# Weight sums of the last era made ahead of the spectral stage, query tiles kept from gate sums to output, and spectral visits that begin with five free banks

## The chip, the cores and the metric

The kernel runs on one core of a Trainium2 chip. The metric is the device time of one execution in microseconds (us). Before the change the median of three runs is 385.83 us (385.55 to 385.86). The engines are PE (the matrix engine), DVE, ACT and POOL (vector, activation and general engines) and SP, whose queue issues nearly all transfers.

## What is computed

One sequence of S = 2048 tokens with D = 512 channels, in fp32. Cut to what matters:

```python
def _A_ref(q, k, v, shift_k, ssm_k, ssm_D):
    for t in range(4):                                   # short causal convolution of k
        k_shift += pad(k, 3)[:, t:t + S, :] * shift_k[:, 3 - t]
    kv = k_shift * v
    y = irfft(rfft(pad(kv, S)) * rfft(pad(ssm_k, S)))[:S]    # long convolution, length 2 S
    return q * (y + kv * ssm_D)

def _B_ref(x, w1, w2):                                   # w1 512 x 1792, w2 1792 x 512
    return relu(x @ w1) @ w2

x = A_q
g = sigmoid((x * gate_w).sum(-1, keepdims=True))         # one gate per token
return g * _A_ref(x, ...) + (1 - g) * _B_ref(x, w1, w2)
```

## The kernel before

**Two halves on one PE.** The MLP (`_B_ref`) takes most of PE's time. A product in fp32 is made of three matmuls: each operand is split into a high part (an ACT cast) and a low part (`split`, L300 to L312: the low part is one subtraction on DVE, or on POOL), and high x high, high x low and low x high are added up in PSUM. Of `mlp1` these are L385 to L387 (m<-xh/xl, w0), of `mlp2` L607 to L609 (m<-w1, hh/hl). A dense matmul takes 128 partitions and 512 columns. The 14 blocks of the hidden width are worked in three eras (blocks 0 to 4, 5 to 9, 10 to 13), each over four chunks of 512 tokens; the partial output of an era is kept in y tiles (L617, L622). The last era makes `x @ w1` by a seven-product scheme (`combine`: products X, V and Y in L458 to L460). It needs sums of quarters of the inputs (t1 to t4, L408, tiles r_b and xs_b) and of the weights: s1 = a21+a22, s2 = s1-a11, s3 = a11-a21, s4 = a12-s2, made by `load_combined` (L543, tiles raw_s) and split like any weight (w0l_l_s; the last quarter a22 in L562).

**The convolution** is a transform in two levels, in 64-row matmuls on tiles of PE that stand between the dense ones as "visits". Eight visits of stage 1 (L652) write the array sa in device memory. Then come the spectral visits (`conv_mid`): visit g reads group g of sa and has, in this order, the inverse of group g-2 (iv, L839, four PSUM banks), the transform of the filter (f_h, two and two banks) and of the signal (f_x, two and two banks; L765). There are eight, and two more (here iv6 and iv7) that have the inverse alone. ACT copies iv out (bv, L849, then stored to sb) and half of f_h (L792); DVE makes the other half of ha from f_h (L797), multiplies it with f_x (p of 2048 columns, then ha, qa, qb, ha of 1024 columns, L805), and POOL adds these products into p (L811, eight sums of 512 columns a group; four of group 7 on DVE). p is what the inverse reads two visits later. Four visits of `conv_end` (cy, L918) read sb, and `after` and `finish` (L928, L864) multiply by q and the gates, add y and store the output.

**Gates.** `gates` loads q a second time in eight tiles gq of 512 KB and makes sixteen row sums with one DVE instruction each (L883), then one sigmoid on ACT and 1-g on DVE. This happens during stage 1; the spectral stage's memory opens only when it is over. `conv_end` loads each q tile once more (tag q), and the output has tiles o.

**What sets the order.** Nothing is ordered by the hardware. `Plan` collects all instructions with a duration, a rank, the buffers and PSUM banks (eight, called cv) that they take and give, and plays them through; the order in which it starts them is written out, and each engine runs its list in that order. A DVE or POOL instruction that waits therefore holds all that stand behind it on its engine, and a PE matmul that waits for a bank holds PE. A visit is a chain on PE that nothing may enter. Its first link starts in the plan if it can take its own banks; a `need` asks for more free banks than it takes, for at most PATIENT = 20 us of the plan, and only the cy visits use it (NEED = 4):

```python
if op["need"] and not live and op["asked"] > now - PATIENT and op["need"] > sum(o is None or o.get("over", False) for o in line["cv"]):
    continue
```

The iv link of every visit carries `pair` 4, whose patience is 0 (LONG), so it starts with the four banks that it takes. Ring r has eight tiles of 512 KB, used in turn by loads of stage 1, of the spectral groups, of the first half of the last era's inputs and of sb.

Of the kernel before, what the change touches and what calls it, by code (L numbers as in the profile page):

```python
# [14 lines left out]
P = 128  # L15
NF = DFF // P
NCHUNK = 4
NJ = 32
# [53 lines left out]
class Plan:  # L72
# [24 lines left out]
    def order(self):  # L97
# [157 lines left out]
def build(tc, wf, xp, qn, kn, vn, hn, dn, sh, gw, w1, w2, cs1, ccf, cci, cib, out):  # L255
# [12 lines left out]
    sb = dram.tile([P, 32, D], F32, name="sb")  # L268


    room = {"raw": RAW, "x": 4, "cv": 8, "hh": HB, "o": OB, "cc": BEHIND + 1, "cf": 2, "qa": 1, "qb": 1, "acc": ACC, "tmp": TMP, "ev": EV, "r": RB,
            "ha": HAB, "p": PB, "bv": BVB, "j": 1, "q": QB, "w1": WA, "w2": WB, "xs": 4, "gq": 2}
# [123 lines left out]
    def combine(p, c, d, cgate):  # L396
        pairs = [tuple(ERAS[2][2 * u:2 * u + 2]) for u in range(2)]
        rank = (1, XR[p])
        tag = "xs" if p else "r"
        raws, made = {}, {}  # L400
        for nm, src, k0 in (("b22", d, 2), ("b12", d, 0), ("b11", c, 0), ("b21", c, 2)):
            go = lambda nm=nm, src=src, k0=k0: nc.sync.dma_start(rows(tile_of(("xc", p, nm), tag, 2 * D, p=cpool[0] if p else mp)), xp[src, k0:k0 + 2].rearrange("k p d -> p k d"))
            raws[nm] = add("SP", ISSUE, (-47, rank[1])[p], go, [cgate if p else xgate[0]], [tag], dma=2 * ROW, fifo=[tag])
# [27 lines left out]
        def again():  # L431
            nc.sync.dma_start(rows(tile_of(("xc", p, "b22"), "xs", 2 * D)), xp[d, 2:4].rearrange("k p d -> p k d"))

        for nm, ld in (("t2", "t4"), ("t3", "t2"), ("t4", "t4"), ("t1", "t2"), ("b22", None)):
            if not ld:
                made[ld] = add("SP", ISSUE, rank[-1], again, [cgate, made["t2"]], ["xs"], dma=2 * ROW, fifo=["xs"])
            for i in range(2):
                cut(nm, i, made[ld], [tag if ld else "xs"] if i else [])
# [80 lines left out]
        begun[0] = p5[1]  # L519
# [4 lines left out]

    def load_combined(rank):
        tt = lambda eng: (nc.gpsimd if eng == "POOL" else nc.vector).tensor_tensor
        H = 256
        for u in range(2):
            f, g = ERAS[2][2 * u], ERAS[2][2 * u + 1]
            lf = loaded(("w", 0, f), w1[f], rank - 3 + u, mp)  # L530
            lg = loaded(("w", 0, g), w1[g], rank - 3 + u, mp)
            T["wr", u] = f, g
            own = split(("w", 0, f), "w0", (1, rank + u), lf, WA, wp, ["w1"], ())[1]
            wpart["a11", u] = wpart["a12", u] = own
            ops = {}

            def combo(nm, half, a, b, sign, deps, take=(), give=(), u=u):
                def go(eng="DVE"):
                    key = ("wc", "s12" if nm in ("s1", "s2") else "s34", u)
                    if take:  # L540
                        tile_of(key, "raw", p=mp)
                    part = lambda q: T["w", 0, T["wr", u][q[0]]][:, H * q[1]:H * q[1] + H] if len(q) == 2 else T["wc", "s12", u][:, H * q[0]:H * q[0] + H]
                    tt(eng)(T[key][:, H * half:H * half + H], part(a), part(b), op=OP.add if sign > 0 else OP.subtract)  # L543

                return add("DVE", dve_time(H), (1, rank + u), go, deps, take, give, port=True, alt=("POOL", 0.68), fifo=take)
# [6 lines left out]
            hi, lo = ("wc", "h", "a"), ("wc", "l", "a")  # L552

            def h(u=u, g=g):
                if not u:
                    tile_of(hi, "w0h", dt=F32R, bufs=WA, p=wp)
                nc.scalar.copy(T[hi][:, H * u:H * u + H], T["w", 0, g][:, H:])

            def l(eng, u=u, g=g):
                if not u:  # L560
                    tile_of(lo, "w0l", dt=F32R, bufs=WA, p=wp)
                tt(eng)(T[lo][:, H * u:H * u + H], T["w", 0, g][:, H:], T[hi].bitcast(F32)[:, H * u:H * u + H], op=OP.subtract)  # L562

            for nm, ld in (("s34", s4), ("a", s3), ("s12", s4)):
                if nm == "a":
                    a = add("ACT", act_time(H), (1, rank + u), h, [lg, ahigh[0]], [] if u else ["w1"], fifo=[] if u else ["w1"])
                    ahigh[0] = a
                    wpart["a22", u] = add("DVE", dve_time(H), (1, rank + u), l, [a, s3, alow[0]], (), ["raw"], port=True, alt=("POOL", 0.68))
                    alow[0] = wpart["a22", u]
                else:  # L570
                    own = split(("wc", nm, u), "w0", (1, rank + u), ld, WA, wp, ["w1"], ["raw"])[1]
                    for q in nm[1:]:
                        wpart["s" + q, u] = own

    ahigh, alow = [None], [None]
# [172 lines left out]
    def conv_mid(g, gate):  # L748
# [6 lines left out]
        def link(dur, fn, deps, take, give=(), pair=0):  # L755
            o = add("PE", dur, (0, rank), fn, (deps if not chain else [chain[-1]]), take, give, tiles=True, pair=pair)
            chain.append(o)
            return o
# [16 lines left out]
        for o in [old]:  # L775
            if o >= 0:
                put_iv(o, link(2 * TILES, lambda o=o: inverse(o), deps, ["cv"] * 4, ["p", "cc"], 4))
        if g >= NJ // 4:
            plan.chain(chain)
            return  # L780
        planes = lambda z, u, n=2: T[k(z)][:, u * D:(u + n) * D].rearrange("p (r d) -> p r d", d=D)
        ha, fh = [], []
        for o in range(2):
            f = link(TILES, lambda o=o: rounds("h", o), deps, ["cv"] * 2 + ([] if o else ["ha"]), rtags[g, "h"] if o else ())
            fh.append(f)

# [68 lines left out]
    def finish(n, key, rank, deps, give):  # L855
        parts = 2 if n == LAST else 1
        prev = None
        for i in range(parts):
            z = slice(i * D // parts, (i + 1) * D // parts)

            def go(z=z):
                if z.start == 0:
                    tile_of(("o", n), "o")
# [3 lines left out]
            prev = add("DVE", dve_time(D // parts) + 0.06, (*rank, i), go, deps + [prev], [] if i else ["o"], give if last else (), port=n // 4 not in DIRECT)  # L867
            add("SP", ISSUE, 0, lambda z=z: nc.sync.dma_start(out[:, n, z], T["o", n][:, z]), [prev], (), ["o"] if last else (), dma=ROW // parts)
# [4 lines left out]
    def gates():  # L873
        gwl = add("SP", ISSUE, GATE - 3, lambda: nc.sync.dma_start(tile_of(("gwt",), "gwt"), gw.partition_broadcast(P)), [sload[0]], dma=ROW)
        prev = []
        for n in range(0, 16, 2):
            key = ("gq", n)
# [213 lines left out]
```

## Time and profile before

| | before |
|---|---|
| median of three runs | 385.83 us |
| the profiled execution, its own time | 385.63 us |
| its span (first to last instruction) | 383.9 us |
| PE busy | 377.8 us, 2481 matmuls |
| DVE, ACT, POOL busy | 298.6, 170.2, 89.4 us |
| bytes moved | 99.84 MB |

The time of the profiled execution is its span and 1.7 us around it. Each row of the timeline gives the start from the span's beginning, the duration, engine, line, operation, output<-input, and the shape; rows "x32" join one stretch of equal matmuls. Matmuls overlap, so the distance from start to start is what one of them costs, not its duration. In brackets stands idle time of the engine before the row and what ended it.

### The profile page before, as it was taken

Reading aid. Unit: us, or ns where it says so; the run is one execution under the profiler, and the core shown is the slowest. Engines: PE = TensorE matmul, PEld = TensorE weight load, DVE = VectorE, ACT = ScalarE, POOL = GpSimd, SP = SyncE. Lnnn points to the kernel's source line nnn. Section 1 sums busy time; section 2 is a strip of 40 time slices with the busy share of each in tenths; the row PEclk is TensorE's granted clock in tenths of the full one; section 3 lists DMA queues with packets and bytes.
Section 4 is the critical chain, followed back from the end, with each engine's and each line's share of the span. In section 5 each row is a group of like instructions: output and inputs, shape, how many; then the busy total and the mean of one; then the engine's idle time right before and its main releaser. Section 6 shows DMA issues by size and latency. Waiting matters only on the chain.

```text
span 383.9 us, 6643 instructions
## 1 busy us (share of the span) xinstructions
PE 377.8 (98%) x2481; PEld 269.7 (70%) x2481; DVE 298.6 (78%) x383; ACT 170.2 (44%) x311; POOL 89.4 (23%) x71
## 2 busy tenths in 40 slices
PE   9999999999999999999999999989999999999995
PEld 5888877877877876886645565565778887668864
DVE  5698999999699774258878987999987718979262
ACT  5642356176156547142134253324228854268410
POOL 1000000000000000000988899969620000000000
PEclk9999999999999999999999999999999999999999
DMA  8999388878968959998777998782057991889303
GB/s 275 383 317 295 131 306 305 323 271 294 339 248 299 316 228 335 304 400 244 249 284 269 311 320 280 235 290 111 8 174 267 384 387 40 281 324 325 114 27 109
DMA packets 46194, 99.84 MB, mean 260 GB/s; under 512 B 4785, under 2 KB 7361, under 8 KB 46162
## 3 DMA queue, kind: packets, MB, share of 16 engines
q1 hardware_dynamic: 45810, 99.11, 73.8%
q8 instruction: 19, 0.31, 0.3%
q10 hardware_dynamic: 288, 0.26, 0.2%
q14 instruction: 13, 0.11, 0.1%
q0 software_dynamic: 64, 0.05, 0.1%
HBM read 70.04 MB, written 29.36 MB: 259 GB/s over the span
## 4 chain that ended last, share of the span: by engine, by line
PE 93%; DVE 4%; DMA 1%; issue 1%; DVEq 0%; ACT 0%
PE m L607 13%; PE m L609 13%; PE m L608 13%; PE m L385 9%; PE m L387 9%; PE m L386 9%; PE f_h L765 4%; PE iv L839 4%; PE m L371 3%; PE f_x L765 3%; PE s1x L652 2%; PE X L458 2%; PE cy L918 2%; PE X L460 2%; PE X L459 2%; PE s1h L652 2%
## 5 line engine op out<-in xcount | busy, mean ns | idle before, releaser
L607 PE MATMUL m<-w1h_h,hh 128*128 128x512 f32 x224 | 89.1, 398 | 0.0
L608 PE MATMUL m<-w1l_l,hh 128*128 128x512 f32 x224 | 87.3, 390 | 0.0
L609 PE MATMUL m<-w1h_h,hl 128*128 128x512 f32 x224 | 87.3, 390 | 0.0
L811 POOL TENSOR_TENSOR p<-p,ha 128x512 f32<-128x512 f32 x30 | 40.1, 1358 | 190.2 <-DMA cf<-ccf 179.5
L607 PEld LDWEIGHTS m<-w1h_h,hh 128*128 128x128 f32 x224 | 42.0, 188 | 21.4 <-issue 6.7
L581 ACT ACTIVATE hh<-m 128x512 fp32r<-128x512 f32 x40 | 23.6, 599 | 71.7 <-PE m L387 71.7
L609 PEld LDWEIGHTS m<-w1h_h,hl 128*128 128x128 f32 x224 | 42.1, 188 | 9.0
L608 PEld LDWEIGHTS m<-w1l_l,hh 128*128 128x128 f32 x224 | 42.1, 188 | 8.3
L584 DVE SCALAR_TENSOR_TENSOR hl<-m,hh 128x512 fp32r<-128x512 f32 x40 | 27.2, 687 | 18.3 <-ACT hh L581 18.2
L385 PE MATMUL m<-xh_h,w0h_h 128*128 128x512 f32 x96 | 37.9, 395 | 1.1 <-DVE ha L797 1.1
L387 PE MATMUL m<-xh_h,w0l_l 128*128 128x512 f32 x96 | 37.4, 390 | 0.0
L386 PE MATMUL m<-xl_l,w0h_h 128*128 128x512 f32 x96 | 37.4, 389 | 0.0
L622 ACT COPY y<-m 128x512 f32<-128x512 f32 x28 | 16.5, 590 | 41.3 <-PE m L609 41.1
L849 ACT COPY bv<-iv 128x512 f32<-128x512 f32 x32 | 17.6, 596 | 33.9 <-PE iv L839 26.2
L711 DVE TENSOR_TENSOR acc<-acc,tmp 128x1024 f32<-128x1024 f32 x24 | 29.4, 1224 | 0.7
L385 PEld LDWEIGHTS m<-xh_h,w0h_h 128*128 128x128 f32 x96 | 18.0, 188 | 8.5 <-issue 2.5
L811 POOL TENSOR_TENSOR p<-p,qb 128x512 f32<-128x512 f32 x16 | 23.0, 1464 | 0.4 <-DVE qb L805 0.4
L708 DVE TENSOR_TENSOR tmp<-r,sht_sht 128x512 f32<-128x512 f32 x32 | 20.9, 684 | 1.1 <-DMA r<-kn 1.1
L387 PEld LDWEIGHTS m<-xh_h,w0l_l 128*128 128x128 f32 x96 | 18.0, 188 | 3.8
L386 PEld LDWEIGHTS m<-xl_l,w0h_h 128*128 128x128 f32 x96 | 18.0, 188 | 3.6
L805 DVE TENSOR_TENSOR ha<-f_x,ha 128x1024 f32<-128x1024 f32 x16 | 19.5, 1219 | 0.6
L657 ACT COPY ev<-s1x 128x512 f32<-128x512 f32 x32 | 16.4, 600 | 6.0 <-PE s1x L652 6.0
(145 smaller groups left out, 655.2 us busy)
## 6 DMA issues: line engine op xcount, KB each, us to landing
sa<-ev SPq DMA_DIRECT2D x64, 256.0 KB, 2.7
r_h<-sa SPq DMA_DIRECT2D x16, 512.0 KB, 5.7
r_x<-sa SPq DMA_DIRECT2D x16, 512.0 KB, 6.9
sb<-bv SPq DMA_DIRECT2D x32, 256.0 KB, 2.6
r<-sb SPq DMA_DIRECT2D x16, 512.0 KB, 6.8
raw<-xp SPq DMA_DIRECT2D x28, 256.0 KB, 3.7
raw<-w SPq DMA_DIRECT2D x24, 256.0 KB, 3.5
r<-kn SPq DMA_DIRECT2D x10, 512.0 KB, 6.1
```

The lines of the kernel that those rows point to most:

```text
L385: mm(ps, part("h", f, k), T["x", "h", xe, c, k], start=k == 0, stop=False)
L386: mm(ps, part("h", f, k), T["x", "l", xe, c, k], start=False, stop=False)
L387: mm(ps, part("l", f, k), T["x", "h", xe, c, k], start=False, stop=k == 3)
L581: nc.scalar.activation(tile_of(("hh", era, c, f), "hh", dt=F32R, p=mp, bufs=HB), T["m1", era, c, f], AF.Relu)
L584: nc.vector.scalar_tensor_tensor(tile_of(("hl", era, c, f), "hl", dt=F32R, p=mp, bufs=HB), T["m1", era, c, f], 0.0, T["hh", era, c, f].bit ...
L607: mm(ps, T["hh", era, c, f][:, z], T["w", "h", 1, f], start=f == fs[0] and not seeding, stop=False, skip_group_check=True)
L608: mm(ps, T["hh", era, c, f][:, z], T["w", "l", 1, f], start=False, stop=False, skip_group_check=True)
L609: mm(ps, T["hl", era, c, f][:, z], T["w", "h", 1, f], start=False, stop=f == fs[-1], skip_group_check=True)
L708: nc.vector.tensor_tensor(o[:, z], T["k", c + (j == 0) + part][:, u], T["sht",][:, j * D:(j + 1) * D], op=OP.mult)
L711: nc.vector.tensor_tensor(T["acc", c], T["acc", c], T[dst], op=OP.add)
L765: mm(ps[b][32 * j:32 * j + 32, :], T[k("cf")][at, 64 * j + 32 * o:64 * j + 32 * o + 32], T[k("r", t, j // 2)][at, (j % 2) * D:(j % 2 + 1) ...
L811: (nc.gpsimd if eng == "POOL" else nc.vector).tensor_tensor(planes("p", dst, n), planes("p", dst, n), planes(src, u, n), op=OP.add if sign ...
```

## The change

Three edits, and what the plan makes of them.

**1. Weight sums early.** `combine_w` loads each pair of blocks of the last era into a tile of ring r, makes the four sums in another one on DVE (eight instructions of 256 columns in all) and stores them to tw in device memory, during stage 1. `load_combined` (rank 512 instead of 535) then loads six ready tiles (two plain blocks, two of s1 and s2, two of s3 and s4) and a seventh with the two quarters a22, and each is split as one tile of 512 columns.

**2. Gates late, q kept.** `gates` gets rank 690, in the last era. Its eight loads of q go to ring r and stay there: the row sums read them, and `after` and `finish` work in them in place and store the output from them. The tiles gq, q and o are gone; the unused product of the row sum goes to qa, the gate weights to qb, both free after the last spectral group. There are two sigmoids, of eight columns each. The loads of sb get a ring of their own (br). The spectral stage no longer waits for the gates to open; phase 3 of the plan (cy visits, second half of the inputs) does.

**3. Five banks.** The first link of a spectral visit has `need` 5 (NEEDM), 4 where it has the inverse alone. Besides, all eight sums of group 7 and two of group 6 are made on DVE.

```diff
@@ Plan.order
             if op["pair"]:
                 event(now + LONG[op["pair"] - 1] + 0.01, "wake", op)
+            if op["need"]:
+                event(now + PATIENT + 0.01, "wake", op)
@@ combine
-            raws[nm] = add("SP", ISSUE, (-47, rank[1])[p], go, ...
+            raws[nm] = add("SP", ISSUE, -47, go, ...
...
-        begun[0] = p5[1]
+        begun[0] = (p5 if LATE[p] else y)[1]
+    def combine_w(u, rank):
...
+        deps = [add("SP", ISSUE, rank - 3, ld, (), ["r"], dma=2 * ROW, fifo=["r"])]
+        q = lambda key, i: T[key][:, i * H:(i + 1) * H]
+        for dst, a, b, sign in ((0, (raw, 2), (raw, 3), 1), (2, (raw, 0), (raw, 2), -1), (1, (new, 0), (raw, 0), -1), (3, (raw, 1), (new, 1), -1)):
...
+            deps = [add("DVE", dve_time(H), (1, rank), go, deps, ...
+        wready[u] = add("SP", ISSUE, (-5000, rank), lambda: nc.sync.dma_start(tw[u], T[new]), deps, (), ["r"], dma=2 * ROW)
@@ load_combined
-            s1 = combo("s1", 0, (1, 0), (1, 1), 1, [lg], ["raw"])
-            s3 = combo("s3", 0, (0, 0), (1, 0), -1, [lf, lg, own], ["raw"])
-            s2 = combo("s2", 1, (0,), (0, 0), -1, [s1, lf])
-            s4 = combo("s4", 1, (0, 1), (1,), -1, [s2, s3], (), ["raw"])
+        for u in range(2):
+            wpart["a11", u] = wpart["a12", u] = load(("w", 0, f + 2 * u), [w1[f + 2 * u]])
+        for u in range(2):
+            wpart["s1", u] = wpart["s2", u] = load(("wc", "s12", u), [tw[u][:, :D]], [wready[u]])
+        for u in range(2):
+            wpart["s3", u] = wpart["s4", u] = load(("wc", "s34", u), [tw[u][:, D:]], [wready[u]])
+        wpart["a22", 0] = wpart["a22", 1] = load(("wc", "a"), [w1[f + 1][:, H:], w1[f + 3][:, H:]])
@@ conv_mid
-            o = add("PE", dur, (0, rank), fn, ..., tiles=True, pair=pair)
+            o = add("PE", dur, (0, rank), fn, ..., tiles=True, pair=pair, need=0 if chain else NEEDM if g < NJ // 4 else 4)
@@ finish
-                nc.vector.scalar_tensor_tensor(T["o", n][:, z], T[key][:, z], gs(2, n), T["q", n][:, z], op0=OP.mult, op1=OP.add)
+                nc.vector.scalar_tensor_tensor(T["q", n][:, z], T[key][:, z], gs(2, n), T["q", n][:, z], op0=OP.mult, op1=OP.add)
@@ gates
+        gwl = add("SP", ISSUE, GATE - 1, weights, ys[7], ["qb"], dma=ROW)
+        j = add("SP", 0.0, GATE - 1, junk, ys[7], ["qa"])
...
+                    ld = add("SP", ISSUE, GATE, load, [gate], ["r"], dma=2 * ROW, fifo=["r"])
...
+                prev.append(add("DVE", dve_time(D) + 0.08, rank, go, [ld, gwl, j, *prev[-1:]], port=True))
@@ build
-    p2 = add("SP", 0.0, -1e3, lambda: phase(2), stores["h"] + stores["x"] + [gdone])
+    p2 = add("SP", 0.0, -1e3, lambda: phase(2), stores["h"] + stores["x"])
...
+    gates(m2[1, CHUNKS[1][-1], 1])
+    p3 = add("SP", 0.0, -1e3, lambda: phase(3), sbstores + [gdone[n] for n in order_n])
@@ constants
-NEED, PATIENT = 4, 20.0
+NEED, NEEDM, PATIENT = 4, 5, 20.0
+XW = 512.0
+PREP = 42.0, 43.0
-DSUM = {7: (2, 3, 6, 7)}
-GATE = 45.0
+DSUM = {7: tuple(range(8)), 6: (6, 7)}
+GATE = 690.0
+BR = 8
+LATE = True, False
```

The plan moves instructions all over the program. Three places matter for what follows. The numbers behind the names count tiles as they are allotted, and differ between the two programs; f_h_1_6 is a bank of group 6's filter transform, m_1_1_9 the bank of hidden block 9 for chunk 1 in the second era.

DVE between the products of group 5 and those of group 6, before: four weight sums (L543) and a split of a weight (L310) stand between them.

```order
L805 TENSOR_TENSOR ha_2559<-f_x_1_5_2582,ha_2559 128x1024
L543 TENSOR_TENSOR raw_s_0_2679<-raw_11_2532 128x256
L310 TENSOR_TENSOR w0l_l_10_2681<-raw_10_2528,w0h_h_10_2591 128x512
L543 TENSOR_TENSOR raw_s_0_2679<-raw_s_0_2679,raw_10_2528 128x256
L543 TENSOR_TENSOR raw_s_0_2700<-raw_10_2528,raw_11_2532 128x256
L543 TENSOR_TENSOR raw_s_0_2700<-raw_10_2528,raw_s_0_2679 128x256
L797 TENSOR_TENSOR ha_2713<-f_h_1_6_2704,ha_2713 128x512
L797 TENSOR_TENSOR ha_2713<-f_h_1_6_2684,ha_2713 128x512
L805 TENSOR_TENSOR p_2754<-f_x_0_6_2720,ha_2713 128x2048
```

The same place after.

```order
L807 TENSOR_TENSOR qb_2630<-f_x_1_5_2557,ha_2552 128x1024
L614 TENSOR_TENSOR y_7_710<-m_1_1_3_2602,y_7_710 128x512
L807 TENSOR_TENSOR ha_2552<-f_x_1_5_2574,ha_2552 128x1024
L799 TENSOR_TENSOR ha_2698<-f_h_1_6_2689,ha_2698 128x512
L799 TENSOR_TENSOR ha_2698<-f_h_1_6_2674,ha_2698 128x512
L807 TENSOR_TENSOR p_2735<-f_x_0_6_2704,ha_2698 128x2048
```

The five instructions are gone from here; the split of block 10 now stands on POOL, and further splits (of s1 to s4 and of a22) stand on POOL between the sums of group 6, which were alone there before:

```order
L813 TENSOR_TENSOR p_2589<-p_2589,ha_2552 128x512 x2
L313 TENSOR_TENSOR w0l_l_s_0_2757<-raw_s_0_2447,w0h_h_s_0_2747 128x512
L813 TENSOR_TENSOR p_2735<-p_2735,ha_2698 128x512
L313 TENSOR_TENSOR w0l_l_s_1_2789<-raw_s_1_2457,w0h_h_s_1_2771 128x512
L813 TENSOR_TENSOR p_2735<-p_2735,ha_2698 128x512
L313 TENSOR_TENSOR w0l_l_s_0_2811<-raw_s_0_2519,w0h_h_s_0_2802 128x512
L813 TENSOR_TENSOR p_2735<-p_2735,qa_2776 128x512
L313 TENSOR_TENSOR w0l_l_a<-raw_a,w0h_h_a 128x512
L813 TENSOR_TENSOR p_2735<-p_2735,qa_2776 128x512
L813 TENSOR_TENSOR p_2735<-p_2735,qb_2791 128x512 x2
```

The two sums that are missing in this list of group 6 (its last two) stand on DVE, behind y_0. Behind group 6's products DVE has four input sums of 1024 columns (L412 in the new file) and five hl, one split among them, before it comes to ha of group 7.

DVE after the first Y product of the last era, after the change (nothing of L898 stood here before; hl_1_13 followed hl_1_11 at once): row sums of the gates, of which the first are shown, and eleven of them stand between hl_1_11 and hl_1_13.

```order
L472 TENSOR_TENSOR raw_1_3192<-Y_1_3265,raw_1_3192 128x512
L485 SCALAR_TENSOR_TENSOR hl_1_11_3293<-raw_0_3176,hh_1_11_3283 128x512
L313 TENSOR_TENSOR xl_l_b_1_3300<-r_b_2939,xh_h_b_1_3261 128x512
L898 ISA qa_j,gs_gs<-r_2994,qb_gwt 128x512
L898 ISA gs_gs 128x1
L898 ISA qa_j,gs_gs<-r_3194,qb_gwt 128x512
L898 ISA gs_gs 128x1
```

On PE the number of matmuls and of visits is as before. Ahead of visit 4, PE had 21 dense matmuls since visit 3, the last of them those of block 9, of which a quarter was left for after the visit:

```order
L385 MATMUL m_1_1_9_2331<-xh_h_1_2_1846,w0h_h_9_1164 128x512
L386 MATMUL m_1_1_9_2331<-xl_l_1_2_1860,w0h_h_9_1164 128x512
L387 MATMUL m_1_1_9_2331<-xh_h_1_2_1846,w0l_l_9_1188 128x512
L839 MATMUL iv_2_2350<-p_2166,cc_2031 64x512
L839 MATMUL iv_2_2351<-p_2166,cc_2031 64x512
```

After the change block 9 is complete there, and six matmuls of an mlp2 bank (of its 15) stand ahead of visit 4, 30 since visit 3:

```order
L389 MATMUL m_1_1_9_2295<-xl_l_1_3_1845,w0h_h_9_1147 128x512
L390 MATMUL m_1_1_9_2295<-xh_h_1_3_1817,w0l_l_9_1176 128x512
L604 MATMUL m_1_1_0_2322<-w1h_h_5_1347,hh_1_5_2137 128x512
L605 MATMUL m_1_1_0_2322<-w1l_l_5_1361,hh_1_5_2137 128x512
L606 MATMUL m_1_1_0_2322<-w1h_h_5_1347,hl_1_5_2148 128x512
L604 MATMUL m_1_1_0_2322<-w1h_h_6_1353,hh_1_6_2160 128x512
L605 MATMUL m_1_1_0_2322<-w1l_l_6_1369,hh_1_6_2160 128x512
L606 MATMUL m_1_1_0_2322<-w1h_h_6_1353,hl_1_6_2173 128x512
L841 MATMUL iv_2_2337<-p_2130,cc_1991 64x512
L841 MATMUL iv_2_2338<-p_2130,cc_1991 64x512
```

The heads of other visits move likewise: 30 dense matmuls instead of 27 stand between visits 4 and 5, 63 instead of 30 between 6 and 7, 30 instead of 45 between 7 and iv6; iv7 moves behind more of the last era's X products.

More of the change, by code (lines that the diff above doesn't have):

```diff
@@ L755, in link @@
         def link(dur, fn, deps, take, give=(), pair=0):
-            o = add("PE", dur, (0, rank), fn, (deps if not chain else [chain[-1]]), take, give, tiles=True, pair=pair)
+            o = add("PE", dur, (0, rank), fn, (deps if not chain else [chain[-1]]), take, give, tiles=True, pair=pair, need=0 if chain else NEEDM if g < NJ // 4 else 4)
             chain.append(o)
@@ L774, in conv_mid, with turned @@
             deps = last
[L775 to L777 removed]
+        def turned(head=False):
+            if old >= 0:
+                put_iv(old, link(2 * TILES, lambda: inverse(old), deps, ["cv"] * 4, ["p", "cc"], 4 if head else 0))
         if g >= NJ // 4:
[L779 to L780 removed]
+            turned(True)
+            return chain
+        if IV_FIRST:
+            turned(True)
         planes = lambda z, u, n=2: T[k(z)][:, u * D:(u + n) * D].rearrange("p (r d) -> p r d", d=D)
@@ L1036 @@
 TB = 2
-OB = 2
 EV = 6
@@ L1044 @@
 BVB = 4
-QB = 7
 X0 = -31.0
```

157 lines of the change are left out of this document (77 added, 80 removed).

## The prediction

> **What bounds the kernel now.** I read the page first: its busy times and the chain that ended last.
>
> ```profile
> span 383.9 us, 6643 instructions
> PE 377.8 (98%) x2481; PEld 269.7 (70%) x2481; DVE 298.6 (78%) x383; ACT 170.2 (44%) x311; POOL 89.4 (23%) x71
> PE 93%; DVE 4%; DMA 1%; issue 1%; DVEq 0%; ACT 0%
> ```
>
> PE is busy 98% of the span, the next engine 78%. So the time is what PE's list costs, and a change can gain only by taking idle time or stretched matmuls off PE. Then the waits, PE's alone:
>
> ```profile
> PE m L385 <- DVE ha L797: 1.1, 1, 1.1
> PE warm L942 <- PEq L1084: 0.8, 1, 0.8
> PE m L371 <- ACT w0h_h_g L342: 0.2, 1, 0.2
> ```
>
> Two of the three belong to the program's start, which the change doesn't touch. One is left, of 1.1 us. The rest is in the distances from start to start, for which I went to PE's timeline. First dense matmuls, then the iv of visit 6 and the place of the wait behind it:
>
> ```profile
> 224.76 0.39 PE L609 MATMUL m<-w1h_h,hl 128*128 128x512 f32 x1
> 229.54 0.39 PE L609 MATMUL m<-w1h_h,hl 128*128 128x512 f32 x1
> 243.33 1.97 PE L839 MATMUL iv<-p,cc 32*64 32x512 f32 x32
> 249.66 0.40 PE L609 MATMUL m<-w1h_h,hl 128*128 128x512 f32 x1
> 251.17 0.50 PE L385 MATMUL m<-xh_h,w0h_h 128*128 128x512 f32 x1 [1.12 <-DVE ha L797]
> ```
>
> The first two rows are 21 matmuls apart: 4.78 / 21 = 0.228 us each. The last two are neighbours and 1.51 apart: **1.28 us lost**.
>
> Now the spectral visits. The first row of each pair is the visit's iv, the second the first dense matmul behind it:
>
> ```profile
> 206.85 1.97 PE L839 MATMUL iv<-p,cc 32*64 32x512 f32 x32
> 212.35 0.50 PE L385 MATMUL m<-xh_h,w0h_h 128*128 128x512 f32 x1
> 217.34 2.38 PE L839 MATMUL iv<-p,cc 32*64 32x512 f32 x32
> 223.50 0.50 PE L385 MATMUL m<-xh_h,w0h_h 128*128 128x512 f32 x1
> 229.86 1.97 PE L839 MATMUL iv<-p,cc 32*64 32x512 f32 x32
> 235.62 0.50 PE L607 MATMUL m<-w1h_h,hh 128*128 128x512 f32 x1
> 257.53 2.05 PE L839 MATMUL iv<-p,cc 32*64 32x512 f32 x32
> 263.94 0.50 PE L385 MATMUL m<-xh_h,w0h_h 128*128 128x512 f32 x1
> 274.39 2.22 PE L839 MATMUL iv<-p,cc 32*64 32x512 f32 x32
> 276.54 0.50 PE L607 MATMUL m<-w1h_h,hh 128*128 128x512 f32 x1
> 285.61 1.97 PE L839 MATMUL iv<-p,cc 32*64 32x512 f32 x32
> 287.51 0.50 PE L458 MATMUL X<-xh_h,w0h_h 128*128 128x512 f32 x1
> ```
>
> The same 96 matmuls take 5.50 us in visit 3, 6.16 in visit 4, 5.76 in visit 5 and 6.41 in visit 7; the inverse alone takes 2.15 (iv6) and 1.90 (iv7). A visit takes twelve banks and there are eight, so its later links wait for the copies of its own iv; what lies above 5.76 is something else, and DVE's timeline shows it:
>
> ```profile
> 217.53 0.68 DVE L584 SCALAR_TENSOR_TENSOR hl<-m,hh 128x512 fp32r<-128x512 f32 x1
> 259.87 0.68 DVE L584 SCALAR_TENSOR_TENSOR hl<-m,hh 128x512 fp32r<-128x512 f32 x1
> ```
>
> In visits 4 and 7 the iv was already running (217.34, 257.53) when DVE had still to read a bank of an earlier block: the visit began with the last bank that it could take.
>
> **Edit 1, the sums of the weights.** DVE's rows ahead of the wait:
>
> ```profile
> 243.31 1.24 DVE L543 TENSOR_TENSOR raw_s<-raw 128x256 f32<-128x256 f32 x1
> 244.47 1.77 DVE L310 TENSOR_TENSOR w0l_l<-raw,w0h_h 128x512 fp32r<-128x512 f32 x1
> 249.01 1.51 DVE L543 TENSOR_TENSOR raw_s<-raw,raw_s 128x256 f32<-128x256 f32 x1
> 250.44 1.28 DVE L797 TENSOR_TENSOR ha<-f_h,ha 128x512 f32<-128x512 f32 x2
> 283.81 0.41 DVE L543 TENSOR_TENSOR raw_s<-raw 128x256 f32<-128x256 f32 x1
> ```
>
> Five instructions hold DVE from 243.31 to 250.44. They leave, and ha can run when f_h is there. What is late next? An undisturbed visit shows when ha runs by itself:
>
> ```profile
> 233.91 1.36 DVE L797 TENSOR_TENSOR ha<-f_h,ha 128x512 f32<-128x512 f32 x2 [2.03 <-PE f_h L765]
> ```
>
> That is 4.05 after the visit's iv (229.86), done by 5.41. PE asked for ha's bank at 249.66 + 0.23 = 249.89, 6.56 after the iv of visit 6 (243.33). Cover 1.15 us: the whole 1.28 goes. The eight sums cost DVE in stage 1 at most 8 x 0.41 = 3.3 us, where sixteen row sums leave (11.7, below); PE shows no wait there, so I take 0.
>
> The 1.24 to 1.51 us against 0.41 for the same 256 columns is POOL's sums running beside. The Trainium skill, "SBUF — State Buffer", section "Who interferes with whom", says that a vector instruction with two SBUF inputs contends with a GpSimd instruction that reads SBUF, and that the loser blocks for the other's whole length. These rows agree: 1.51 is 0.41 and most of one POOL sum. That rule speaks against part of this change, which puts six splits on POOL and more input sums on DVE beside them; by it they would block each other as the sums did. What that would cost is rival (c).
>
> **Edit 3, five banks.** With one bank more at the head, an hl that is still due frees a bank that f_h takes, not iv. I take 5.76 for visits 4 and 7, the length of visit 5: 0.40 + 0.65; and 1.90 for iv6, as for iv7: 0.25. **Sum 1.30.** The order of bank uses within visits 2, 4, 5, 6 and 7 is that of the 5.76 visits; only visit 3 has the other. Ends: 0, if the plan's free bank is not free on the chip; and 2.60, if all five also come down to 5.50 (5 x 0.26 = 1.30 more). A visit that waits for five banks does not leave PE idle: the plan puts dense matmuls ahead of it (30 instead of 21 before visit 4), of which there are as many as before.
>
> What the moved work could cost, by margins. The tightest in the stretch is between visits 6 and 7, where DVE has, behind ha of group 6, the products, five hl, four input sums and a split:
>
> ```profile
> L805 DVE TENSOR_TENSOR ha<-f_x,ha 128x1024 f32<-128x1024 f32 x16 | 19.5, 1219 | 0.6
> L805 DVE TENSOR_TENSOR p<-f_x,ha 128x2048 f32<-128x2048 f32 x8 | 18.3, 2290 | 0.7
> L584 DVE SCALAR_TENSOR_TENSOR hl<-m,hh 128x512 fp32r<-128x512 f32 x40 | 27.2, 687 | 18.3 <-ACT hh L581 18.2
> L408 DVE TENSOR_TENSOR r_b<-r_b,r_b x4: 1208/1890/2200, 260.5 to 266.7; 128x1024 f32<-128x1024 f32 x4
> ```
>
> 5.41 + 2.29 + 4 x 1.22 + 5 x 0.69 + 4 x 1.89 + 1.77 = 25.4 us after the iv of visit 6. PE comes to visit 7 at 5.76 + 63 x 0.228 = 20.1 and asks for ha's first bank 6.56 later, at 26.7. Slack 1.3; with all four input sums at the longest, 2.20, it is 0.1. Rows overlap by some 0.08 (243.31 + 1.24 against the next start, 244.47), so I take 0 and keep +1 as an end. POOL's sums of group 6 with four splits between them are ten instructions of 1.36 (alone) to 2.2:
>
> ```profile
> L811 POOL TENSOR_TENSOR p<-p,ha 128x512 f32<-128x512 f32 x30 | 40.1, 1358 | 190.2 <-DMA cf<-ccf 179.5
> L562 POOL TENSOR_TENSOR w0l_l_a<-raw,w0h_h_a 128x256 fp32r<-128x256 f32 x1 | 2.2, 2192 | 4.5 <-ACT w0h_h_a L557 4.5
> ```
>
> The first product that they read is done 5.41 + 2.29 + 0.69 + 1.22 = 9.6 after the iv of visit 6, so POOL ends at 23 to 32. DVE comes to the group's last two sums, behind ha, p and y_0 of visit 7, at 20.1 + 5.41 + 2.29 + 0.69 = 28.5, and behind them stand the y sums that free banks for iv6. Most of POOL's sums run at 1.36, so again 0, with an end of +3.5.
>
> **Edit 2, the gates.** Two row sums in succession, and the line of the tile gq on its loads:
>
> ```profile
> 165.28 0.69 DVE L883 CUSTOM_DVE_ANT_0 j<-gq,gwt_gwt 128x512 f32<-128x512 f32 x1
> 166.01 0.69 DVE L883 CUSTOM_DVE_ANT_0 j<-gq,gwt_gwt 128x512 f32<-128x512 f32 x1
> DMA to landing us min/median/max: 4.4/6.3/10.0
> ```
>
> 0.73 from one to the next, sixteen are 11.7 us, and the tile's loads landed within 4.4 to 10.0. Eleven stand ahead of hl_1_13. From t0, the end of the first Y products: three instructions ahead of them at 0.69, 11 x 0.73 and hl_1_13's own 0.69 make 10.8. PE asks for it after 48 mlp2, 12 Y and 5 more matmuls, 65 x 0.228 = 14.8: hidden, slack 4.0. Behind the row sums wait the sums of the second Y products (made 60 matmuls, 13.7 us, after t0) and hl_1_12: two DVE instructions and an ACT copy between them end near 16.0, and PE asks for it after 77 matmuls, at 17.5. The last q load can go only when DVE has read its ring tile (about t0 + 2.4), and its row sum stands nine row sums later, 6.3 after the issue, exactly the median landing; at the longest landing of 10.0 (12.4 after t0) two row sums, hl_1_13, one more row sum, two Y sums, hl_1_10 and hl_1_12 follow, 3 x 0.73 + 5 x 0.69 = 5.6, and hl_1_12 is half a us late. I take 0, with an end of +2. The earlier removal of the 4 MB of q in stage 1 gives PE nothing, since it did not wait there. The writing of tw and its loads (1 MB each) are far ahead of their use. The outputs' end, the last mlp2 and the store behind it, keeps its form: 0.
>
> **Sum:** 1.28 + 1.30 = 2.58 us. The profiled execution took 385.63, so 383.05; the median of the runs lies 0.20 above the profiled one, so **383.2**.
>
> **The rivals.**
>
> (a) *The visits keep their length.* The plan's free banks come from its own durations, and its head already had four by that account while an hl was still to come. Then only the 1.28 is gained: 385.83 - 1.3 = 384.5. Small new stalls of up to 1.8 us on a full gain end in the same place (383.6 to 385.0). Against it: one bank is 0.5 us or more of reading. Chance 0.20.
>
> (b) *The visits come down to 5.50 too*: 383.2 - 1.3 = 381.9. For it speaks only visit 3, whose order of banks the others don't have. Chance 0.06.
>
> (c) *The contention moves with the work* and DVE or POOL hold PE between visits 6 and 7 by 2 us or more: 385.2 to 386.4, about the time before. For it: the slack of 1.3, the rule quoted, and r_b at 2.20. Chance 0.12.
>
> (d) *Slower: the last q load.* PE waits at m of hl_1_12, in the last era, if the load lands more than 9.5 us after its issue (17.5 - 5.6 - 2.4); the gain is eaten at 12.1, and beyond 12.9 the kernel is slower by over 0.2%. At 15 it costs 5.5 us: 383.2 + 5.5 = 388.7. Against it: 10.0 is the longest of eight. For it: the q loads come on top of the last era's own loads. Chance 0.10, with what else may go over.
>
> (e) That the change doesn't do what it says is excluded for the order, which shows the sums gone from the spectral stage and the heads moved.
>
> **How the numbers follow.** My forecast (gain 2.1 to 3.1) has 0.52, (b) 0.06, (a) 0.20, (c) 0.12, (d) 0.10. 0.2% is 0.77 us, about what a measurement of this kernel can tell. Faster by more than that: the first three, 0.78; within: (c), 0.12; slower: 0.10. The range goes from 381.9, (b), to 385.6, the lower part of (c); left out are (d) and half of (c), 0.16.
>
> **What would show it.** Right: PE's waits have no row on ha (L799 in the new file); iv to dense is 5.76 or less in visits 4 and 7 and 1.90 in iv6; start to start of dense matmuls stays at 0.228 from visit 6 to 8. Wrong: a row "PE m <- DVE hl" or "<- DVE ha" of over 1 us; a visit of 6 us; POOL's splits at 2 us between group 6's sums with PE idle behind; row sums of the gates that wait for r<-qn.

## The result and the profile after

The changed kernel takes 383.68 us in the median, against 385.86 us for the kernel before on the same chip: a ratio of 0.9937, with a 95% interval of 0.9925 to 0.9949. That is 2.2 us less; 383.2 us was predicted. One of the five executions of the changed kernel took 473.29 us at a granted clock of 0.754, and the ratio is that of the others. The profiled execution has a span of 381.9 us against 383.9.

The page of the changed kernel, its busy times and its chain, and the rows of PE in its waits:

```profile
span 381.9 us, 6628 instructions
PE 377.1 (99%) x2481; PEld 270.1 (71%) x2481; DVE 299.0 (78%) x387; ACT 169.9 (44%) x311; POOL 82.4 (22%) x67
PE 99%; DVE 0%; DVEq 0%; issue 0%
```

```profile
PE warm L957 <- PEq L1107: 0.8, 1, 0.8
```

The wait of 1.1 us on ha is gone, and the chain is PE from end to end. PE's timeline of the changed kernel, with the iv of visit 4, of visit 7 and iv6, each with the first dense matmul behind it:

```profile
220.12 1.97 PE L841 MATMUL iv<-p,cc 32*64 32x512 f32 x32
225.88 0.50 PE L604 MATMUL m<-w1h_h,hh 128*128 128x512 f32 x1
266.69 1.97 PE L841 MATMUL iv<-p,cc 32*64 32x512 f32 x32
272.44 0.50 PE L604 MATMUL m<-w1h_h,hh 128*128 128x512 f32 x1
279.49 1.97 PE L841 MATMUL iv<-p,cc 32*64 32x512 f32 x32
281.39 0.50 PE L604 MATMUL m<-w1h_h,hh 128*128 128x512 f32 x1
```

5.76, 5.75 and 1.90 us, where there were 6.16, 6.41 and 2.15: the three lengths forecast, 1.31 us together. The idle time of 1.28 took 0.11 more with it, since the first matmul behind a gap cost 0.335 to the next start (251.17 before) and not 0.228. So 2.70 us went where the prediction said. The span shows 2.0, and two places give back the rest. One is the last bank of a stage 1 visit (the first two rows below are another one, for comparison):

```profile
122.24 1.06 PE L649 MATMUL s1h<-r,s1c_s1t 32*64 32x512 f32 x16
123.23 0.50 PE L604 MATMUL m<-w1h_h,hh 128*128 128x512 f32 x1
...
144.77 1.26 PE L649 MATMUL s1h<-r,s1c_s1t 32*64 32x512 f32 x16
145.96 0.50 PE L604 MATMUL m<-w1h_h,hh 128*128 128x512 f32 x1
```

1.19 instead of 0.99: 0.20 lost. By the order of the two lists, that bank is freed by DVE's addition to a y tile, which runs from 144.21 to 144.90; in the new order four splits stand directly ahead of it on DVE, three before. The other place is the program's first matmuls, whose order is the same in both kernels. Before:

```profile
4.34 0.73 PE L371 MATMUL m<-xh_h,w0h_h_g 128*128 128x512 f32 x2 [0.17 <-ACT w0h_h_g L342]
5.95 0.62 PE L371 MATMUL m<-xl_l,w0h_h_g 128*128 128x512 f32 x2
```

After:

```profile
4.34 1.29 PE L374 MATMUL m<-xh_h,w0h_h_g 128*128 128x512 f32 x2
6.52 0.62 PE L374 MATMUL m<-xl_l,w0h_h_g 128*128 128x512 f32 x2
```

They begin together, and the fourth pair starts 0.57 later, because the first matmuls still cost about twice as much as later ones: in the changed kernel the second pair starts 1.09 us behind the first (at 5.43), in the kernel before 0.58 (at 4.92). The trace's record of the granted clock begins, with 1.0, at 3.43 us in the kernel before and at 5.76 in the changed kernel; ahead of that it has no entry. In the fourteen profiles of this case the 41st matmul (the nine of the warm-up counted) starts at 11.6 to 12.5 us, in the same program up to there; the kernel before had the earliest of all. The Trainium skill, "TensorE: Matmul & The Clock Gate", Part 1, says that the clock doubles after a window of activity that runs freely and doesn't start with the kernel, so that the turn falls at another place in each run. The traces agree with a spread of 0.8 us. So 2.70 - 0.20 - 0.57 = 1.93 us, about the difference of the spans.

### The profile page after: what moved, and what is told of

Its sections match the earlier page's. It is cut to its first block, busy times and chain, and to the rows that moved or that the text cites. A ratio compares the mean times of both kernels' runs of the same rounds, so it can differ in the third digit from the quotient of the medians.

```text
span 381.9 us, 6628 instructions
## 1 busy us (share of the span) xinstructions
PE 377.1 (99%) x2481; PEld 270.1 (71%) x2481; DVE 299.0 (78%) x387; ACT 169.9 (44%) x311; POOL 82.4 (22%) x67
## 4 chain that ended last, share of the span: by engine, by line
PE 99%; DVE 0%; DVEq 0%; issue 0%
PE m L604 14%; PE m L606 13%; PE m L605 13%; PE m L388 9%; PE m L390 9%; PE m L389 9%; PE iv L841 4%; PE f_x L762 4%; PE f_h L762 4%; PE m L374 3%; PE s1x L649 2%; PE X L462 2%; PE cy L933 2%; PE X L463 2%; PE X L464 2%; PE s1h L649 2%
## 5 line engine op out<-in xcount | busy, mean ns | idle before, releaser
L813 POOL TENSOR_TENSOR p<-p,ha 128x512 f32<-128x512 f32 x26 | 33.1, 1296 | 184.8 <-DVE ha L807 184.3
L799 DVE TENSOR_TENSOR ha<-f_h,ha 128x512 f32<-128x512 f32 x16 | 10.6, 688 | 12.6 <-PE f_h L762 11.6
L813 POOL TENSOR_TENSOR p<-p,qa 128x512 f32<-128x512 f32 x14 | 20.2, 1464 | 0.0
```

Of the source, the lines that this page charges most:

```text
L813: (nc.gpsimd if eng == "POOL" else nc.vector).tensor_tensor(planes("p", dst, n), planes("p", dst, n), planes(src, u, n), op=OP.add if sign ...
```

## The experiments

Ratios are to the kernel before, on the same chip, with 95% intervals; each of the three groups of four kernels had its own runs of the kernel before (medians 385.97, 386.02 and 385.97).

| kernel | median us | ratio |
|---|---|---|
| e1_four_banks | 385.16 | 0.9973 (0.9964 to 0.9982) |
| e2_only_five_banks | 386.04 | 0.9995 (0.9986 to 1.0004) |
| e3_only_weight_sums | 393.32 | 1.0187 (1.0169 to 1.0205) |
| e4_six_banks | 394.97 | 1.0229 (1.0215 to 1.0243) |
| e5_late_sums | 385.72 | 0.9992 (0.9983 to 1.0001) |
| e6_gates_twice | 391.94 | 1.0154 (1.0140 to 1.0168) |
| e7_no_sums_same_order | 383.55 | 0.9943 (0.9931 to 0.9956) |
| e8_four_banks_other_ranks | 385.66 | 0.9987 (0.9978 to 0.9996) |
| e9_four_banks_seed_early | 385.61 | 0.9989 (0.9980 to 0.9997) |
| e10_splits_on_dve | 385.12 | 0.9973 (0.9964 to 0.9981) |
| e11_seven_ev | 383.62 | 0.9935 (0.9923 to 0.9948) |
| e12_seven_ev_four_banks | 384.50 | 0.9960 (0.9947 to 0.9972) |

My theory: the gain is 1.4 us from the sums' leaving DVE and 1.3 us from the five banks, and late gates cost nothing. The rival: the five banks do nothing for the visits, which are long only because DVE is late.

**e1_four_banks.**

```diff
-NEED, NEEDM, PATIENT = 4, 5, 20.0
+NEED, NEEDM, PATIENT = 4, 4, 20.0
```

> The changed kernel, but a spectral visit may begin with the four banks that its inverse takes, as before; the rest (weight sums early, gates late) stays, and the order of all engines is made anew. My theory (five free banks at the head take a visit from 6.2 to 6.4 down to 5.76): two or more spectral visits read over 5.9 us from iv to the next dense matmul or iv6 reads 2.15, and the time is 0.4 to 1.3 us above the changed kernel's, 384.1 to 385.0; no idle row on ha. Rival (the rule buys nothing, the visits are shorter only because DVE is freer without weight sums): all visits 5.76 or less, time as the changed kernel's, 383.7.

PE's timeline, visits 4 and 7 and a matmul of the last mlp2:

```profile
217.91 1.97 PE L841 MATMUL iv<-p,cc 32*64 32x512 f32 x32
223.66 0.50 PE L388 MATMUL m<-xh_h,w0h_h 128*128 128x512 f32 x1
257.69 1.97 PE L841 MATMUL iv<-p,cc 32*64 32x512 f32 x32
263.45 0.50 PE L388 MATMUL m<-xh_h,w0h_h 128*128 128x512 f32 x1
367.68 0.50 PE L604 MATMUL m<-w1h_h,hh 128*128 128x512 f32 x1 [0.55 <-ACT m L598]
```

The time is 1.5 us above the changed kernel's, a little more than my theory had, and for another reason. With four banks asked for the visits take 5.75 and 5.76 and iv6 1.91, as in the changed kernel. In this order, though, DVE is done with the last hl 0.2 us ahead of the iv of visits 4 and 7 (at 217.72 and 257.50), while in the kernel before an hl was still due. So the run shows that five banks need not be asked for in this order; it doesn't show what a late hl does to a visit with four. The 1.5 us are elsewhere: 0.3 in visit 3 (5.76, not 5.50), 0.8 where PE waits for ACT's copy of y into the banks of the last mlp2 (the seed copy), the rest in small waits. In the changed kernel the same copies are hidden, because the last cy visit stands between the second Y products and that mlp2:

```profile
364.54 0.39 PE L464 MATMUL Y<-xh_h_b,w0l_l_s 128*128 128x512 f32 x1
364.86 1.95 PE L933 MATMUL cy<-br,ibt_ibt 64*32 64x512 f32 x32
366.74 0.50 PE L604 MATMUL m<-w1h_h,hh 128*128 128x512 f32 x1
```

**e2_only_five_banks.** The kernel before with the third edit alone (without its sums on DVE):

```diff
+            if op["need"]:
+                event(now + PATIENT + 0.01, "wake", op)
...
+            o = add("PE", dur, ..., pair=pair, need=0 if chain else NEEDM if g < NJ // 4 else 4)
```

> The kernel before with the rule of five free banks alone. My theory: all spectral visits from 4 on read 5.76 or less and iv6 1.90, which is worth 1.3 us; three weight sums still stand on DVE between the products of groups 5 and 6, so that an idle of about 0.4 to 1.4 us on ha may stay: 384.3 to 385.0. Rival (the rule needs the freer DVE of the other edits): visits above 5.9 remain, 385.5 or more.

The visits are short here too (visit 4 5.76, visit 7 5.81, iv6 1.91) and there is no wait on ha, yet nothing is gained. Visit 7, on PE and on DVE:

```profile
258.62 1.97 PE L841 MATMUL iv<-p,cc 32*64 32x512 f32 x32
264.43 0.50 PE L387 MATMUL m<-xh_h,w0h_h 128*128 128x512 f32 x1
260.96 0.68 DVE L586 SCALAR_TENSOR_TENSOR hl<-m,hh 128x512 fp32r<-128x512 f32 x1
```

DVE is as late here as in the kernel before: its last hl begins 2.34 us behind the iv in both (260.96 here, 259.87 before). With five free banks asked for the visit takes 5.81 all the same, not 6.41. That speaks for the rule; it is one visit, and in another order of ACT's copies.

One wait of PE is new, in the last era:

```profile
PE X L460 <- ACT raw L476: 1.2, 1, 1.2
```

ACT's copy of an X product stands behind a cast that waits for PE. With its second start the wait costs 1.5 us, smaller ones between 272 and 274 us some 0.6, and this profile has the slowest start of all (0.8 us). So the rule alone removes the long visits as well, and its new order puts waits of its own elsewhere.

**e3_only_weight_sums.** The kernel before with the first edit alone: `combine_w` and the new `load_combined`, its rank 528.

> The kernel before with the weight sums ahead of the spectral stage alone (the loads of the sums at rank 528, gates early as before, visits begin with four banks). My theory: the idle of 1.3 us on ha and the 0.1 of starting again go; the visits keep lengths of 5.5 to 6.4; 384.5. With sums and row sums both in stage 1, DVE has 2.7 us more there, which costs PE nothing. Rival: stage 1 becomes late by them, PE waits at the first spectral visit or at hl, and the time is that of before or more, 385.8 to 387.

```profile
PE X L459 <- ACT xh_h_b L308: 2.4, 1, 2.4
PE X L460 <- DVE xl_l_b L311: 0.8, 1, 0.8
PE iv L833 <- DVE hl L482: 0.7, 1, 0.7
```

The idle on ha is gone, as both had it, and the rival's harm is larger than it said. Row sums and weight sums both stand in stage 1, ahead of the spectral stage's memory: 1-g, the end of the gates, comes at 176.04 instead of 168.25, and the first visit at 183.9 us, 9 us later than in the kernel before. The last inverse is then late, and with it the inputs that may be loaded only behind it. The two waits on them, 3.6 us with what the next starts lose, are followed by thirteen matmuls at 0.43 us, another 2.6, and iv6 takes 2.7 longer, waiting for an hl. So the first edit, as tried here, needs the second; e1, which has both and four banks, takes 8 us less. That gates stand late isn't a gain of its own but makes room for the sums.

**e4_six_banks.**

```diff
-NEED, NEEDM, PATIENT = 4, 5, 20.0
+NEED, NEEDM, PATIENT = 4, 6, 20.0
```

> The changed kernel with six free banks asked for at the head of a spectral visit. My theory (the length of a visit falls with the banks that are free at its head, 6.4 with four, 5.76 with five): 5.50 in most of the six visits, 0.26 each, so 1.0 to 1.6 us less, 382.1 to 382.7, if the later heads do not make the end of the spectral stage late. Rival: the heads go later by some 9 dense matmuls each, the last inverse and cy wait, and the time is the changed kernel's or more, 383.7 to 386.

```profile
PE X L462 <- ACT xh_h_b L310: 4.7, 1, 4.7
PE m L604 <- DVE ha L799: 3.0, 2, 1.6
```

The rival was right in kind and too mild. Two visits fall to 5.50, but up to visit 6 each head has 3 to 12 dense matmuls more ahead of it, iv6 36 and iv7 51; the last inverse comes 25 us later (322.7), and the inputs behind it are late by 4.7 us, with a slow clock after it. Two waits on ha, behind visits 3 and 7, make 3.0 more. Five is not a step on a way that goes on.

**e5_late_sums.** The changed kernel with the old `load_combined(535)` and without `combine_w`.

> The changed kernel with the weight sums made in the spectral stage again (as in the kernel before); gates late and five free banks stay. If the sums ahead are worth what my prediction gave them, PE has an idle of about 1 to 1.4 us on ha or on an s weight between visits 5 and 7 again, and the time is 0.8 to 1.6 us above the changed kernel's: 384.5 to 385.3. Rival (once the heads are moved, the sums collide with nothing, as in the run with five banks alone, which had no wait on ha): within 0.4 us of the changed kernel's, 383.3 to 384.1.

PE behind visit 7 and DVE's row of that time:

```profile
264.02 0.39 PE L389 MATMUL m<-xh_h,w0l_l 128*128 128x512 f32 x1
265.76 0.50 PE L387 MATMUL m<-xh_h,w0h_h 128*128 128x512 f32 x1 [1.35 <-DVE ha L805]
```

```profile
258.97 6.14 DVE L411 TENSOR_TENSOR r_b<-r_b,r_b 128x1024 f32<-128x1024 f32 x3
```

The time is 2.0 us above the changed kernel's. The wait on ha is back, 1.5 us, but what stands directly ahead of ha is not a weight sum: three input sums of 2.05 us each hold DVE beside POOL's sums. Alone such a sum takes 1.2 (xs_b). The weight sums still have a part in it that was not separated: behind them ha of group 6 starts 4.98 us after its iv instead of 4.05, and from there to the late ha DVE has no pause over 0.1 us. The wait on the seed copy is there as well (0.6 on the waits page). It comes with five banks as it does in e1 with four, and the last cy visit stands ahead of the second Y products in both (362.23 here, 360.88 in e1). Which instruction comes last ahead of ha is up to the order.

**e6_gates_twice.**

```diff
+                    for _ in range(2):
-                    nc.vector.tensor_tensor_reduce(T["j",][:, :D], T["q", n], ...)
+                        nc.vector.tensor_tensor_reduce(T["j",][:, :D], T["q", n], ...)
```

> The changed kernel with each row sum of the gates made twice, in the same order on every engine (the second one writes the same result). My theory (eleven row sums ahead of hl_1_13 have 4 us of cover): they take 8.1 us more there, PE waits about 4.0 us at hl_1_13 and about 1.3 at hl_1_12, and the time is 5.3 us above the changed kernel's, 389. Rival (the cover is wider, since the inputs of the last era's second half or others are late anyway): 1 us or less above, 384.7.

PE's timeline, and the stretch of 4.1 us behind the wait in a table by window (its seventh number is the granted clock):

```profile
319.40 0.39 PE L605 MATMUL m<-w1l_l,hh 128*128 128x512 f32 x1
324.86 0.80 PE L606 MATMUL m<-w1h_h,hl 128*128 128x512 f32 x1 [5.06 <-DVE hl L485]
325.45 0.63 PE L604 MATMUL m<-w1h_h,hh 128*128 128x512 f32 x1
325.88 0.63 PE L605 MATMUL m<-w1l_l,hh 128*128 128x512 f32 x1
```

```profile
324.90:329.00 4.10, 4.10 (x10) 3.23 (x11) 4.07 (x11) 1.42 (x4) 0.00 (x0) 0.50 0.41 123
```

8.3 us are lost. The wait at hl_1_13 is there, 5.2 us from start to start against 4.0 expected: I had left out the row sums ahead of the first Y products, which are doubled too. A seed copy is late by another 0.9. The remaining 2.1 us I had not expected: after the gap PE's clock is granted at 0.50, and eight matmuls behind the first take 0.43 us each.

**e7_no_sums_same_order.** The kernel before, in its own order:

```diff
-                    tt(eng)(T[key][:, H * half:H * half + H], part(a), part(b), op=OP.add if sign > 0 else OP.subtract)
+                    nc.vector.memset(T[key][:, H * half:H * half + H], 0.05)
```

> The kernel before in its own order on every engine, but the eight weight sums are replaced by fills of the same 256 columns, which read nothing (the sums are left out, the last era's weights are not the reference's). My theory of the prediction: the idle on ha goes, 1.4 us with its second start, and visits 4 (6.16) and 7 (6.41) keep their length, since their heads begin with four banks: 384.5. Rival that the run with four banks suggests (a freer DVE alone shortens the visits): visit 7 comes down to 5.76 as well, 383.9; visit 4 lies ahead of the sums and stays in both.

PE's timeline, visits 4 and 7, and DVE's last hl ahead of visit 7's later banks:

```profile
217.54 2.38 PE L839 MATMUL iv<-p,cc 32*64 32x512 f32 x32
223.70 0.50 PE L385 MATMUL m<-xh_h,w0h_h 128*128 128x512 f32 x1
256.34 1.97 PE L839 MATMUL iv<-p,cc 32*64 32x512 f32 x32
262.11 0.50 PE L385 MATMUL m<-xh_h,w0h_h 128*128 128x512 f32 x1
257.11 0.68 DVE L584 SCALAR_TENSOR_TENSOR hl<-m,hh 128x512 fp32r<-128x512 f32 x1
```

This separates the two. Nothing is moved, no fifth bank is asked for, and the time is that of the changed kernel. The idle goes (1.4), visit 7 falls from 6.41 to 5.77 and iv6 from 2.15 to 1.91: 2.3 us come from the sums' leaving alone. Visit 4, ahead of the sums, stays at 6.16. The long visit 7 was an echo of the same delay: its last hl begins 0.77 us behind the iv here and 2.34 before. By an estimate, most of the delay was not the sums' own work: at the 0.41 us that a sum takes alone (at 283.81 before) and with the split at 1.24 as here, the five instructions that began at 243.31 would have been over near 246.2, ahead of f_h, for which ha waits until 247.61 here; beside POOL's sums they lasted until 250.44. The run takes away both the work and the collision and doesn't part them.

**e8_four_banks_other_ranks.** e1 with two more numbers changed:

```diff
-XW = 512.0
+XW = 510.0
-BACK = 1.5
+BACK = 2.0
```

> The changed kernel with four free banks at the heads, as in e1_four_banks, and in another order (rank of the weight loads 510 instead of 512, the first products of the last era taken 0.5 ranks earlier). If e1 lost its 1.5 us to the rule, this one loses as much or more, by a wait of its own near the end of the spectral stage or in the last era: 385 to 386.5, with visits of 5.5 to 5.8 again. Rival (e1's wait on the seed copy was an accident of one order): 383.7 to 384.3.

2.0 us above the changed kernel, visits 5.76 to 5.81, and the same wait on the seed copy (0.6), with another on ACT's copy of an X product (0.5). So a second order with four banks has e1's loss. The number of banks alone doesn't decide it, since e5 has the same wait with five.

**e9_four_banks_seed_early.** e1 with:

```diff
-LATE = True, False
+LATE = True, True
```

> The run with four free banks (e1_four_banks) with one thing more: the copies that seed the banks of the last mlp2 may be made after the first Y product, as in the kernel before, instead of after the second. Theory after the first runs (the rule of five banks does not shorten the visits; it is worth 1.5 us because with it the last cy visit stands behind the second Y products and covers these copies, 0.8 us, and the rest is small waits): the wait of PE m on ACT m is gone and the time is 0.8 us under e1's, 384.3. My prediction's theory (the rule pays in the visits): nothing changes, 385.2.

The wait is gone and PE's last matmul starts at 377.66, 0.83 earlier than in e1 (378.49), but the time doesn't fall. The last cy visit, then the last DVE piece of the chain:

```profile
373.15 1.95 PE L933 MATMUL cy<-br,ibt_ibt 64*32 64x512 f32 x32
```

```profile
379.52 0.48 DVE r L864
```

Now the last cy visit stands too near the end. Eight steps of 0.7 us on DVE follow it, and DVE ends last: the span ends 5.8 us after PE's last start, not 4.4. In the changed kernel the same visit begins at 364.86, 12.7 us ahead of PE's last start.

**e10_splits_on_dve.** `split(..., both=False)` for the last era's weights, so that their six low parts leave POOL.

> The changed kernel with the six splits of last-era weights that stand on POOL put on DVE. My prediction's term (0 for POOL's splits): within 0.4 us of the changed kernel's, 383.3 to 384.1, and no wait on ha or hl in either. Rival (c) of the prediction (splits on POOL block DVE's sums, and PE feels it): 0.5 to 1.5 us faster than the changed kernel. The opposite rival (DVE's list becomes too long behind group 6): PE waits for ha of group 7 by 1 to 3 us.

```profile
PE f_h L762 <- DVE ha L807: 1.3, 1, 1.3
```

```profile
235.32 1.48 DVE L313 TENSOR_TENSOR w0l_l<-raw,w0h_h 128x512 fp32r<-128x512 f32 x1
236.72 1.21 DVE L807 TENSOR_TENSOR ha<-f_x,ha 128x1024 f32<-128x1024 f32 x1
```

1.4 us slower than the changed kernel, by the opposite rival, though behind group 4 and not group 6: a split stands ahead of the last product of the group, f_h of visit 5 waits for that, and the visit takes 7.4 us. Here these splits are better on POOL.

**e11_seven_ev and e12_seven_ev_four_banks**, two tries for a better version:

```diff
-EV = 6
+EV = 7
```

and for e12 also four banks and `LATE = True, True`.

> The changed kernel with seven buffers instead of six for the copies of stage 1 (ev), a try for a better version: in the changed kernel one stage 1 visit takes 0.2 us longer, since its last bank waits for an addition to y on DVE, and stage 1's visits could move closer together. Expected 0.2 to 0.6 us less, 383.1 to 383.5, the visits of the spectral stage and their order behind it as before. Rival (the sa stores crowd the loads): same or slower.

> e11 with four free banks at the heads and the early seed copies of e9. If five free banks are worth nothing by themselves (all visits read 5.5 to 5.8 with four, and the seed copy is covered), the time is that of e11 within 0.4 us, 382.9 to 383.5. If the rule still pays, 0.5 us or more above e11.

e11 equals the changed kernel (383.62 and 383.68), so the gain that I expected isn't there: a stage 1 visit still loses 0.3, in another place. e12 is 0.9 us slower than e11. It has the shortest visits of all, three at 5.50 with four free banks, and PE's last matmul starts at 376.79, the earliest; but again the last cy visit is late and the span ends 5.8 us behind that start, at 382.6. No version here beats the changed kernel by more than its interval.

## Why the prediction was right, and where it was not

- **The idle on ha, 1.28 us: right.** Measured 1.28 and 0.11 for the second start, and e7 shows the weight sums as the cause.
- **Five banks, 1.30 us: the size was right, the account only in part.** The step is "with one bank more at the head, an hl that is still due frees a bank that f_h takes, not iv". The changed kernel's visit 4 looks like it: hl begins 0.73 us behind the iv (220.12), and the iv keeps its 1.97 us and the visit 5.76, while before hl began 0.19 us behind the iv, and the iv took 2.38. e2's visit 7 fits it too. What fails is that the prediction gave all of the 1.30 to the banks, beside the sums. 0.89 of it, visit 7 and iv6, come with nothing but the sums gone (e7), so the two terms were not separate. The other 0.40, visit 4, went in every remade order, also with four banks asked for (e1, e8, e9), where hl was over ahead of the iv. I read as too few banks what, by these runs, takes both: a late DVE and no bank to spare.

```profile
220.85 0.68 DVE L581 SCALAR_TENSOR_TENSOR hl<-m,hh 128x512 fp32r<-128x512 f32 x1
```

- **What five banks are worth then.** Next to the other two edits, 1.5 us (e1, in which nothing else is changed); with other numbers changed as well, 1.9 to 2.0 (e8, e9) and 0.9 (e12 against e11). The visits' own lengths make at most 0.3 of e1's 1.5. The most of it is the place of the last cy visit: in the changed kernel it covers the seed copies and leaves DVE 12.7 us to the end; with four banks it fell ahead of the second Y products (e1, e8) or near the end (e9, e12). The place is not tied to the number of banks: e5, with five, has it where e1 has it, and e4, with six, where the changed kernel has it. So this part belongs to the order that the plan happened to make, and the prediction had nothing of it.
- **Rival (a), in which the visits keep their length,** didn't come. That the forecast held although most of the term had another cause that was enough is luck to that extent: with the same rule and the sums left in the stage, e2 gained nothing and e5 0.3 us.
- **The gates at 0: right as a margin, wrong as a value.** hl_1_13 ended at 314.73 and PE came to it at 318.80, 4.07 of cover against 4.0 worked out. The q loads landed within 3.5 to 6.7, so rival (d) was far. But without late gates the first edit, as tried in e3, costs 7 us, so the three edits are not a sum of terms.

```profile
314.04 0.69 DVE L485 SCALAR_TENSOR_TENSOR hl<-raw,hh 128x512 fp32r<-128x512 f32 x1
318.80 0.39 PE L606 MATMUL m<-w1h_h,hl 128*128 128x512 f32 x1
DMA to landing us min/median/max: 3.5/3.8/6.7
```

- **Between visits 6 and 7, slack 1.3: right, with room.** The input sums end at 269.84 and ha of group 7 starts at 270.76, 4.07 after its iv, undisturbed. POOL is done with group 6 at 272.21, and DVE comes to its share at 275.01, 28.6 after the iv of visit 6, where 28.5 was worked out.

```profile
265.56 4.28 DVE L412 TENSOR_TENSOR r_b<-r_b,r_b 128x1024 f32<-128x1024 f32 x2
270.76 1.34 DVE L799 TENSOR_TENSOR ha<-f_h,ha 128x512 f32<-128x512 f32 x2 [0.93 <-PE f_h L762]
```

- **Rival (c), contention,** did not come here, but e5 shows that it was near: the same input sums at 2.05 us stand directly ahead of a wait of 1.5 us there.
- **What was missing:** 0.20 in stage 1, and the start, 0.57 in this pair of profiles, which is why the profile gives less than the sum.

## What to carry to other kernels

When a visit or a block runs long, ask first which engine is behind when it begins: here a late helper engine made its first victim wait openly and the next ones run a little long, and both went when it was freed. When several edits go through one planner, test each by taking the cost away in the old order, since a remade order brings gains and waits of its own. And price a wait on PE by what it does afterwards as well: here the clock fell from waits of 3.1 us in all.

## What the runs showed of the hardware that was not expected

After gaps on PE of 5.1 us (e6), of 2.4 us followed by one matmul and 0.8 us (e3), and of 4.7 us followed by one matmul and 0.6 (e4), the granted clock was 0.50 and matmuls cost 0.43 us instead of 0.228, for some 4 to 6 us; after gaps of 1.1 to 1.6 us (before, e2, e4, e5) it was not. In the traces' record the clock stays down for 6.83 us in each of the three. In e3 it went down within the second gap, with a single matmul between the two, and in e4 behind that matmul too. So in e3 two waits of 3.1 us together cost PE about 6.
